# Attention scores of two tiles as 64 queries by 120 key columns in four array quadrants, in place of 32 queries by 88 columns in eight

## The chip, the cores and the metric

The kernel runs on one core of one Trainium2 chip. The metric is device microseconds (us) from one launch, and the median of several runs is compared. A profiled execution gives a trace beside its time; the time of that execution and its span (first to last instruction) are given below.

## The reference

The program is a block of attention with a local window and block summaries, followed by a feed-forward layer. The batch is 4, there are 8 heads of 64 channels and 768 positions.

```
k_sum = k.reshape(B, H, nb, 32, D).max(axis=3)      # 24 summary keys per head
v_sum = v.reshape(B, H, nb, 32, D).mean(axis=3)
scores_l = scale * q @ k^T                          # kept where |i - j| < 16, else -1e9
scores_s = scale * q @ k_sum^T + log(32)
a = softmax(concat([scores_l, scores_s]))
x = a @ concat([v, v_sum])                          # all heads side by side: 3072 x 512
out = max(x @ w_in, 0)**2 @ w_out                   # 512 -> 2048 -> 512
```

A query sees 31 positions around itself and the 24 summaries. So 64 neighbouring queries need 96 local keys and 24 summaries (120 columns), and 32 neighbouring queries need 64 local keys and 24 summaries (88 columns).

## The kernel before, in words

**Tiles.** The 3072 rows are 24 tiles of 128 queries, six to a batch entry. Two tiles make one of 12 chunks of the feed-forward layer. Heads lie in four pairs: of a pair, one head holds partitions 0 to 63 and the other 64 to 127.

**Two stages.** The text START is an order written out by hand: its tokens are loads, attention steps of tiles 0 to 5, the preparation of the weights (32-bit words split into a high and a low part) and the feed-forward of chunks 0 and 1. Behind START a regular loop runs chunks 2 to 11. A chunk is eight slots. In a slot TensorE does the first product for two blocks of the hidden layer (`ffn1`, L392, 24 matmuls of 256 columns) and then the second product of the two blocks of the slot before (`ffn2`, L433, 12 matmuls of 512 columns). Between the two, ScalarE and VectorE make the square of the positive part in a high and a low piece (`squares`, L400 to L414).

**The attention of the next two tiles is spread over the eight slots** by `period`, which appends each step to the lists `before`, `after` and `last` of a slot. For tiles a and a+1: `softmax` (per head, VectorE subtracts the mask and takes the maximum, L307, and ScalarE takes the exponential, L315), `inverse`, `norm` (GpSimd multiplies by the reciprocal sum, four heads in one instruction, L331), `turn` (twelve VectorE transposes of 32-row blocks for each tile, L348). At the end of slot 7 stands what is called a **visit** here: TensorE does `outputs` of both tiles (L362) and the scores of the next two tiles, and `split_x` makes the high and low part of the outputs (ScalarE L376, VectorE L379) for the next chunk's L392.

**Two forms of scores.** Tiles 4 and 5, in START, use `scores` (L254, the matmul's line is 262): for each pair four matmuls, 64 channels by 64 queries by 120 columns, on the four quadrants of the array. Tiles 6 to 23 use `scores_by_group` (L267, the matmul's line is 279): for each pair eight matmuls, 64 channels by 32 queries by 88 columns, on two row halves and four column quarters. Each of these float32 matmuls leaves two records in the trace, each with a weight load of its own. A visit does two tiles, so 64 matmuls, or 128 records. There are nine such visits, the first at the end of START (tiles 6 and 7). The tenth visit has outputs alone.

**Keys.** For tiles from 6 on, a load brings 120 columns per pair and half, of which the middle 24 are room for the maxima; `place_k` writes these from `ksums`. For tiles 4 and 5 the columns lie in five runs of 24, and the maxima are the fifth run. All loads are issued from SyncE in the order of the code.

Of the kernel before, what the change touches and what calls it, by code (L numbers as in the profile page):

```python
# [73 lines left out]
def attn_ffn_kernel(ctx: ExitStack, tc: tile.TileContext, q, k, k0, kt, v, vt, v0, w, masks, gmasks, ident, mean, out):  # L74
# [20 lines left out]
    def by_run(g):
        return k_sb[g % 2].rearrange("a (n s p k) -> a n s p k", n=5, s=2, p=NPAIR)

    def by_pair(g):
        return k_sb[g % 2].rearrange("a (s p k) -> a s p k", s=2, p=NPAIR)
# [154 lines left out]
    def scores(g, p0, p1):  # L254


        if g not in s_ps:
            s_ps[g] = [bank[r].rearrange("a (p k) -> a p k", p=NPAIR) for r in range(2)]
        for p in range(p0, p1):
            for r, s in ((0, 0), (1, 1), (0, 1), (1, 0)):  # L260
                rs, ss = slice(r * 64, r * 64 + 64), slice(s * 64, s * 64 + 64)
                nc.tensor.matmul(  # L262
                    s_ps[g][r][ss, p, 0:NK], lhsT=q_sb[g % 2][rs, s, p, :], rhs=by_run(g)[rs, :, s, p, :],
                    start=True, stop=True,
                )

    def scores_by_group(g):  # L267

        for t in (g, g + 1):
            s_ps[t] = [bank[t % 2 * 2 + r].rearrange("a (p k) -> a p k", p=NPAIR) for r in range(2)]
            for p in range(NPAIR):
                for r, i in ((0, 0), (1, 2), (0, 1), (1, 3), (0, 2), (1, 0), (0, 3), (1, 1)):
                    s, u = divmod(i, 2)
# [1 line left out]
                    nc.tensor.matmul(  # L279
                        s_ps[t][r][i * GQ : i * GQ + GQ, p, 0:GK], lhsT=q_sb[t % 2][rs, s, p, u * GQ : u * GQ + GQ],  # L280
                        rhs=by_pair(t)[rs, s, p, u * GQ : u * GQ + GK], start=True, stop=True,
                    )

    def scores_kt(g, p0, p1):

        if g not in s_ps:
            s_ps[g] = [bank[r].rearrange("a (p k) -> a p k", p=NPAIR) for r in range(2)]
        for p in range(p0, p1):
            for k0, k1 in ((0, 96), (96, NK)):
                for r, s in ((0, 0), (1, 1), (0, 1), (1, 0)):  # L290
# [3 lines left out]
                    nc.tensor.matmul(  # L294
                        s_ps[g][r][ss, p, k0:k1], lhsT=q_sb[g % 2][rs, s, p, :], rhs=keys, start=True, stop=True
                    )

    def mask_max(g, h):

        t = g % NT  # L300
# [6 lines left out]
        nc.vector.tensor_tensor_reduce(  # L307
            out=e_sb[:, h, 0:n], in0=s_ps[g][h % 2][:, h // 2, 0:n], in1=m, scale=-scale, scalar=3.0e38,
            op0=ALU.add, op1=ALU.min, accum_out=nmx[half][:, i : i + 1],
        )  # L310

    def exponentials(g, h):
        half, i = divmod(h, 4)
        e = e_sb[:, h, 0 : NK if g < FROM_GROUPS else GK]
        nc.scalar.activation(e, e, AF.Exp, bias=nmx[half][:, i : i + 1], scale=-1.0, accum_out=sm[half][:, i : i + 1])  # L315
# [12 lines left out]
    def norm(g, half, eng):  # L328
        n = NK if g < FROM_GROUPS else GK
        e = e_sb[:, half * 4 : half * 4 + 4, 0:n]  # L330
        eng.tensor_mul(out=e, in0=e, in1=sm[half].unsqueeze(2).to_broadcast([P, 4, n]))  # L331
# [8 lines left out]
    def turn(g, n0, n1):  # L340

        blocks = [
            (i, c, j) for i in range(4) for c, j in (((0, 0), (32, 1), (64, 3)) if i % 2 == 0 else ((0, 1), (32, 3), (GK - 32, 2)))
        ]
        for i, c, j in blocks[n0:n1]:
            nc.vector.transpose(  # L348
                out=pT[g % 2][j * 32 : j * 32 + 32, :, i * 32 : i * 32 + 32],
                in_=e_sb[i * 32 : i * 32 + 32, :, c : c + 32],  # L350
            )
# [3 lines left out]
    def outputs(g):  # L355
        xp = bank[2 if g < FROM_GROUPS - 1 else free[0] if g < FROM_GROUPS else 5 - g % 2]
        x_ps[g] = xp = xp.rearrange("a (p k) -> a p k", p=NPAIR)

        for s in range(2):
            for h in range(H):  # L360
                o = (h % 2) * 64
                nc.tensor.matmul(  # L362
                    xp[o : o + 64, h // 2, s * 64 : s * 64 + 64],
                    lhsT=v_sb[g % 2][:, s, h * 64 : h * 64 + 64],
                    rhs=pT[g % 2][:, h, s * 64 : s * 64 + 64],
                    start=True, stop=True,
                )
# [168 lines left out]
    def load(what, i):  # L536
# [17 lines left out]
        elif what == "gm":  # L554
            nc.sync.dma_start(out=gmask_sb, in_=gmasks.rearrange("m q c -> q m c"))
        elif what == "id":
            nc.sync.dma_start(out=id_sb, in_=ident)
        else:
            nc.sync.dma_start(out=mean_sb, in_=mean)

    def begin(op, i, j, eng):
# [15 lines left out]
        elif op == "S":  # L577
            if i < FROM_GROUPS:
                (scores_kt if i < FROM_KT else scores)(i, 2 * j, 2 * j + 2)
            else:  # L580
                scores_by_group(i)
# [81 lines left out]
def _group_masks(m):  # L663
    g = np.empty((3, P, GK), np.float32)
    for i in range(P // GQ):
        rows = slice(i * GQ, (i + 1) * GQ)
        runs = [m[:, rows, 0:32], m[:, rows, 32:64], m[:, rows, 64:96]]
        runs = [runs[0], runs[1], m[:, rows, 96:]] if i % 2 == 0 else [runs[1], m[:, rows, 96:], runs[2]]
        g[:, rows] = np.concatenate(runs, axis=2)
    return g  # L670


# [7 lines left out]
def _layouts(q, k, v):  # L680
# [14 lines left out]
    return {
        "q": np.ascontiguousarray(qd).reshape(B, NT, P, 2, NPAIR, 64),
        "k": kg.reshape(B, NT, P, 2 * NPAIR * NK),
        "k0": np.ascontiguousarray(
            kd[0, FROM_KT:].reshape(FROM_GROUPS - FROM_KT, P, 2, NPAIR, 4, NB).transpose(0, 1, 4, 2, 3, 5)
        ),  # L700
# [29 lines left out]
```

## Time and profile before

| what | value |
|---|---|
| median of 3 runs | 624.66 us (624.01 to 625.30) |
| profiled execution | 623.76 us |
| its span | 622.0 us |
| mean granted TensorE clock | 0.992 |
| busy: TensorE matmuls, weight loads | 96%, 86% of the span |
| busy: VectorE, ScalarE, GpSimd | 62%, 43%, 14% |
| bytes moved | 62.33 MB, 100 GB/s |

In the rows below, PE is TensorE's matmul stream and PEld its stream of weight loads, which overlaps the first. DVE is VectorE, ACT ScalarE, POOL GpSimd, SP SyncE. A row of a timeline gives the start, the duration, the engine, the source line, the instruction with its operands, and how many were merged into the row; a bracket at its end is the idle time of the engine just before, and what ended it. "issue" there means that the profile shows nothing for which the engine waited. A row of a group gives the count, then the busy time and the mean of one in ns. A row of windows gives the stretch, its length, and for each engine the busy time with the count of instructions, then the granted clock, the share of the DMA engines and GB/s.

### The profile page before, as it was taken

To read this page: it belongs to the slowest core of one execution; us is meant where nothing else is said; L and a number is where in the kernel's file an instruction comes from. 1 tells how busy PE (TensorE), PEld (TensorE's weight loads), DVE (VectorE), ACT (ScalarE), POOL (GpSimd) and SP (SyncE) were. 2 spreads that over 40 slices of the span, in tenths; PEclk is the share of its full clock that TensorE was granted. 3 is DMA by queue.
4 is the path that set the end of the run, shared out by engine and by line. 5 is a ranking of instruction groups with operands and counts; after the bars stand their busy time and mean duration, and the time that the engine had idled before them with its cause. 6 is when DMAs were issued, how large, how long until landed. Compare 5 with 4: busy or idle time off the path is not lost.

```text
span 622.0 us, 14129 instructions
## 1 busy us (share of the span) xinstructions
PE 595.3 (96%) x5792; PEld 536.8 (86%) x5792; DVE 385.8 (62%) x1073; ACT 266.5 (43%) x706; POOL 89.4 (14%) x83
## 2 busy tenths in 40 slices
PE   2699999999999999999999999999999999999997
PEld 2588888989989999999989988989998998998996
DVE  4889989767645855865653873784763663663221
ACT  2778887333424424425425334334334433332222
POOL 2555762002000000002000000000200000000000
PEclk9979999999999999999999999999999999999999
DMA  8999610545004404203302510600500500200000
GB/s 289 368 355 317 244 70 21 195 161 171 1 2 135 150 3 132 102 2 109 125 2 65 170 52 29 205 1 4 181 2 2 183 0 3 85 2 1 35 1 34
DMA packets 20256, 62.33 MB, mean 100 GB/s; under 512 B 3168, under 2 KB 3296, under 8 KB 18144
## 3 DMA queue, kind: packets, MB, share of 16 engines
q1 hardware_dynamic: 20192, 61.43, 29.8%
q8 instruction: 45, 0.74, 0.5%
q14 instruction: 19, 0.16, 0.1%
HBM read 55.13 MB, written 6.29 MB: 99 GB/s over the span
## 4 chain that ended last, share of the span: by engine, by line
PE 91%; DMA 3%; DVE 2%; ACT 1%; issue 1%; SPq 1%; POOL 0%; DVEq 0%; POOLq 0%
PE o_ps L433 41%; PE ph L392 40%; PE ph L362 3%; PE s_ps L279 2%; PE s_ps L392 2%; DMA w_raw<-in_w 2%; DMA q_sb<-in_q 2%; PE ph L337 1%; PE s_ps L294 1%; PE s_ps L362 1%; DVE w_sb L248 0%; PE o_ps L149 0%; ACT w_sb L123 0%; PE s_ps L262 0%; SPq L172 0%
## 5 line engine op out<-in xcount | busy, mean ns | idle before, releaser
L392 PE MATMUL ph<-xh,w_sb 128*128 128x256 f32 x1448 | 255.8, 279 | 1.5 <-issue 0.9
L433 PE MATMUL o_ps<-w_sb,gh 128*128 128x512 f32 x768 | 238.0, 391 | 0.0
L392 PEld LDWEIGHTS ph<-xh,w_sb 128*128 128x128 f32 x1448 | 225.5, 189 | 9.8 <-issue 1.1
L392 PE MATMUL ph<-xl,w_sb 128*128 128x256 f32 x724 | 201.1, 278 | 0.0
L411 DVE TENSOR_TENSOR ph<-ph,r 128x512 f32<-128x512 f32 (+1 forms) x101 | 64.7, 642 | 152.2 <-ACT r L400 151.6
L433 PEld LDWEIGHTS o_ps<-w_sb,gh 128*128 128x128 f32 x768 | 137.1, 188 | 24.8 <-issue 0.2
L433 PE MATMUL o_ps<-w_sb,gl 128*128 128x512 f32 x384 | 151.4, 394 | 0.8 <-DVE gl L414 0.8
L400 ACT ACTIVATE r<-ph 128x512 f32<-128x512 f32 (+1 forms) x91 | 51.7, 569 | 206.4 <-PE ph L392 206.3
L392 PEld LDWEIGHTS ph<-xl,w_sb 128*128 128x128 f32 x724 | 136.7, 189 | 0.0
L315 ACT ACTIVATE e_sb<-e_sb,nmx 128x88 f32<-128x88 f32 (+1 forms) x192 | 69.8, 365 | 77.3 <-DVE nmx L307 77.3
L348 DVE STREAM_TRANSPOSE pT<-e_sb 32x256 f32<-32x256 f32 x216 | 94.1, 436 | 3.4 <-POOL e_sb L331 0.4
L433 PEld LDWEIGHTS o_ps<-w_sb,gl 128*128 128x128 f32 x384 | 72.3, 188 | 15.6 <-DVE gl L414 1.3
L331 POOL TENSOR_TENSOR e_sb<-e_sb,sm 128x352 f32<-128x352 f32 (+1 forms) x43 | 35.6, 833 | 334.1 <-DVE sm L325 190.3
L414 DVE TENSOR_TENSOR gl<-ph,gh 128x512 fp32r<-128x512 f32 (+1 forms) x101 | 64.2, 636 | 10.5 <-DVE ph L411 0.5
L406 ACT ACTIVATE gh<-r 128x512 fp32r<-128x512 f32 (+1 forms) x112 | 63.9, 571 | 8.7 <-DVE r L402 5.2
L241 POOL TENSOR_TENSOR w_raw<-w_raw 128x1024 int32<-128x1024 int32 x16 | 35.3, 2215 | 24.4 <-ACT w_raw L233 7.5
L315 ACT ACTIVATION_READ_ACCUMULATOR e_sb<-e_sb,nmx 128x1 f32 x192 | 36.0, 188 | 0.0
L307 DVE CUSTOM_DVE_ANT_0 e_sb<-s_ps,gmask_sb 128x88 f32<-128x88 f32 x144 | 27.4, 244 | 0.4
L379 DVE TENSOR_TENSOR xl<-ph,xh 128x512 fp32r<-128x512 f32 x19 | 13.1, 691 | 22.7 <-ACT xh L376 22.7
L324 DVE TENSOR_SCALAR sm<-sm 128x4 f32<-128x4 f32 x48 | 14.9, 311 | 14.7 <-ACT e_sb L315 14.6
L376 ACT CAST xh<-ph 128x512 fp32r<-128x512 f32 x19 | 11.1, 585 | 26.9 <-PE ph L362 26.9
L362 PEld LDWEIGHTS ph<-pT,v_sb 128*64 128x64 f32 x608 | 18.6, 138 | 3.9 <-issue 3.3
(67 smaller groups left out, 394.5 us busy)
## 6 DMA issues: line engine op xcount, KB each, us to landing
w_raw<-in_w SPq DMA_DIRECT2D x16, 1024.0 KB, 13.9
v_sb<-in_v SPq DMA_DIRECT2D x24, 384.0 KB, 5.1
k_sb<-in_k SPq DMA_DIRECT2D x18, 480.0 KB, 6.1
kv<-in_kt SPq DMA_DIRECT2D x16, 384.0 KB, 3.3
q_sb<-in_q SPq DMA_DIRECT2D x24, 256.0 KB, 5.4
out<-ob SPq DMA_DIRECT2D x24, 256.0 KB, 2.1
kv<-in_vt SPq DMA_DIRECT2D x12, 384.0 KB, 4.1
vn<-in_v SPq DMA_DIRECT2D x2, 768.0 KB, 11.0
```

What stands on the lines that cost most here:

```text
L241: nc.gpsimd.tensor_tensor(out=hi, in0=hi, in1=lo, op=ALU.add)
L307: nc.vector.tensor_tensor_reduce(out=e_sb[:, h, 0:n], in0=s_ps[g][h % 2][:, h // 2, 0:n], in1=m, scale=-scale, scalar=3.0e38, op0=ALU.add, ...
L315: nc.scalar.activation(e, e, AF.Exp, bias=nmx[half][:, i : i + 1], scale=-1.0, accum_out=sm[half][:, i : i + 1])
L331: eng.tensor_mul(out=e, in0=e, in1=sm[half].unsqueeze(2).to_broadcast([P, 4, n]))
L348: nc.vector.transpose(out=pT[g % 2][j * 32 : j * 32 + 32, :, i * 32 : i * 32 + 32], in_=e_sb[i * 32 : i * 32 + 32, :, c : c + 32],)
L362: nc.tensor.matmul(xp[o : o + 64, h // 2, s * 64 : s * 64 + 64], lhsT=v_sb[g % 2][:, s, h * 64 : h * 64 + 64], rhs=pT[g % 2][:, h, s * 64 ...
L392: nc.tensor.matmul(ph, lhsT=w_sb[f][:, w, cc * P : (cc + 1) * P], rhs=x[c][:, cc, :], start=(n == 0), stop=(n == 3 * NC4 - 1))
L400: nc.scalar.activation(r, ph, AF.Relu)
L406: nc.scalar.activation(gh, r, AF.Square)
L411: nc.vector.tensor_mul(out=ph, in0=ph, in1=r)
L414: nc.vector.tensor_sub(out=gl, in0=ph, in1=gh.bitcast(F32))
L433: nc.tensor.matmul(o_ps[c][tt], lhsT=g_[:, ts_], rhs=w_sb[f][:, w, DM:], start=(first and n == 0), stop=(last and n == 2),)
```

## The change

`scores_by_group` is gone, and tiles 6 to 23 use `scores`, so that a visit has 32 matmuls of 64 queries by 120 columns (64 records) where it had 64 of 32 by 88 (128 records). The keys of all tiles are loaded in four runs of 24 columns, with the maxima as a fifth run behind them, so a load of keys brings 768 columns where it brought 960. The mask of 88 columns and its load are gone. The maximum, the exponential and the product with the reciprocal work on 120 columns where they worked on 88, and the blocks that `turn` transposes lie at other columns, as many as before. Which banks of PSUM the scores use stays as it was, as does the order of the steps.

```diff
-GQ = 32
-GK = 64 + NB
-FROM_GROUPS = 6
+FROM_PAIRS = 6
...
-KT0 O5 PK6 VT0 PK7 XH5a S6.0 XL5v
+KT0 O5 PK6 VT0 PK7 XH5a S6.0 S6.1 XL5v S7.0 S7.1
...
-    k_sb = [const.tile([P, 2 * NPAIR * NK], F32, name=f"k_sb{i}") for i in range(2)]
+    k_sb = [const.tile([P, 5, 2, NPAIR, NB], F32, name=f"k_sb{i}") for i in range(2)]
...
-        if g < FROM_GROUPS:
-            nc.sync.dma_start(out=by_run(g)[:, 0:4], in_=k0[g - FROM_KT])
-        else:
-            nc.sync.dma_start(out=k_sb[g % 2], in_=k[g // NT, g % NT])
+        nc.sync.dma_start(out=k_sb[g % 2][:, 0:4], in_=k[g // NT, g % NT])
...
-        dst = by_run(g)[:, 4] if g < FROM_GROUPS else by_pair(g)[:, :, :, 64:GK]
-        copy(eng, dst, ksums[g // NT % 2].unsqueeze(1).to_broadcast([P, 2, NPAIR, NB]))
+        copy(eng, k_sb[g % 2][:, 4], ksums[g // NT % 2].unsqueeze(1).to_broadcast([P, 2, NPAIR, NB]))
...
         if g not in s_ps:
-            s_ps[g] = [bank[r].rearrange("a (p k) -> a p k", p=NPAIR) for r in range(2)]
+            n = g % 2 * 2 if g >= FROM_PAIRS else 0
+            s_ps[g] = [bank[n + r].rearrange("a (p k) -> a p k", p=NPAIR) for r in range(2)]
         for p in range(p0, p1):
             for r, s in ((0, 0), (1, 1), (0, 1), (1, 0)):
                 rs, ss = slice(r * 64, r * 64 + 64), slice(s * 64, s * 64 + 64)
                 nc.tensor.matmul(
-                    s_ps[g][r][ss, p, 0:NK], lhsT=q_sb[g % 2][rs, s, p, :], rhs=by_run(g)[rs, :, s, p, :],
+                    s_ps[g][r][ss, p, 0:NK], lhsT=q_sb[g % 2][rs, s, p, :], rhs=k_sb[g % 2][rs, :, s, p, :],
                     start=True, stop=True,
                 )
-    def scores_by_group(g):
-        for t in (g, g + 1):
-            s_ps[t] = [bank[t % 2 * 2 + r].rearrange("a (p k) -> a p k", p=NPAIR) for r in range(2)]
-            for p in range(NPAIR):
-                for r, i in ((0, 0), (1, 2), (0, 1), (1, 3), (0, 2), (1, 0), (0, 3), (1, 1)):
-                    s, u = divmod(i, 2)
-                    rs = slice(r * 64, r * 64 + 64)
-                    nc.tensor.matmul(
-                        s_ps[t][r][i * GQ : i * GQ + GQ, p, 0:GK], lhsT=q_sb[t % 2][rs, s, p, u * GQ : u * GQ + GQ],
-                        rhs=by_pair(t)[rs, s, p, u * GQ : u * GQ + GK], start=True, stop=True,
-                    )
...
         nc.vector.tensor_tensor_reduce(
-            out=e_sb[:, h, 0:n], in0=s_ps[g][h % 2][:, h // 2, 0:n], in1=m, scale=-scale, scalar=3.0e38,
+            out=e_sb[:, h, 0:NK], in0=s_ps[g][h % 2][:, h // 2, 0:NK], in1=m, scale=-scale, scalar=3.0e38,
...
-        e = e_sb[:, h, 0 : NK if g < FROM_GROUPS else GK]
+        e = e_sb[:, h, 0:NK]
...
-        n = NK if g < FROM_GROUPS else GK
-        e = e_sb[:, half * 4 : half * 4 + 4, 0:n]
-        eng.tensor_mul(out=e, in0=e, in1=sm[half].unsqueeze(2).to_broadcast([P, 4, n]))
+        e = e_sb[:, half * 4 : half * 4 + 4, 0:NK]
+        eng.tensor_mul(out=e, in0=e, in1=sm[half].unsqueeze(2).to_broadcast([P, 4, NK]))
...
-            (i, c, j) for i in range(4) for c, j in (((0, 0), (32, 1), (64, 3)) if i % 2 == 0 else ((0, 1), (32, 3), (GK - 32, 2)))
+        blocks = [(i, j) for i in range(4) for j in ((0, 1, 3) if i % 2 == 0 else (1, 2, 3))]
...
-            last[7].append(lambda: scores_by_group(a + 2))
+            last[7] += [lambda g=g: scores(g, 0, NPAIR) for g in (a + 2, a + 3)]
```

How the instructions stand on TensorE at the second visit, before (the end of the last `ffn2`, the outputs of two tiles, the scores of two tiles, the first `ffn1`; the count at a row's end is of matmuls, each of which the trace shows as two records where operands are float32 and not rounded):

```order
L433 MATMUL o_ps<-w_sb,gl 128x512
L362 MATMUL ph<-pT_81,v_sb_76 64x64 x16
L362 MATMUL ph<-pT_82,v_sb_77 64x64 x16
L279 MATMUL s_ps<-k_sb_74,q_sb_78 32x88 x32
L279 MATMUL s_ps<-k_sb_75,q_sb_79 32x88 x32
L392 MATMUL ph<-xh,w_sb 128x256 x2
L392 MATMUL ph<-xl,w_sb 128x256
```

The same place of the changed kernel, where line 398 is `ffn2`, 327 `outputs`, 249 `scores` and 357 `ffn1`:

```order
L398 MATMUL o_ps<-w_sb,gl 128x512
L327 MATMUL ph<-pT_80,v_sb_75 64x64 x16
L327 MATMUL ph<-pT_81,v_sb_76 64x64 x16
L249 MATMUL s_ps<-k_sb_73,q_sb_77 64x120 x16
L249 MATMUL s_ps<-k_sb_74,q_sb_78 64x120 x16
L357 MATMUL ph<-xh,w_sb 128x256 x2
L357 MATMUL ph<-xl,w_sb 128x256
```

The place in the stream is the same; a row of scores holds half as many matmuls, each twice as tall and 120 columns wide. On VectorE at the first visit, the end of START, before (k_sb is written by `place_k`, then come the low part of the outputs and the first maxima of tile 6):

```order
L180 TENSOR_REDUCE ksum_84<-kv 128x24
L123 COPY k_sb_74<-ksum_84 128x8x24
L185 TENSOR_REDUCE vsum<-kv 128x24
L188 TENSOR_SCALAR vsum<-vsum 128x24
L123 COPY k_sb_75<-ksum_84 128x8x24
L379 TENSOR_TENSOR xl<-ph,xh 128x4x128
L307 ISA e_sb,nmx<-s_ps,gmask_sb 128x88
```

And in the changed kernel:

```order
L167 TENSOR_REDUCE ksum_83<-kv 128x24
L113 COPY k_sb_73<-ksum_83 128x192
L172 TENSOR_REDUCE vsum<-kv 128x24
L175 TENSOR_SCALAR vsum<-vsum 128x24
L113 COPY k_sb_74<-ksum_83 128x192
L344 TENSOR_TENSOR xl<-ph,xh 128x4x128
L277 ISA e_sb,nmx<-s_ps,mask_sb 128x120
```

Here too the places are the same; the copies write one run where they wrote eight pieces, and the maxima read 120 columns.

More of the change, by code (lines that the diff above doesn't have):

```diff
@@ L63 @@
 F1.19 CA14a GL17v MU18 LO15a GL18v F1.20 SU14v RE19a F2.17 SQ19 AD15 MU19 CA13a GL19v RE20v F2.18 E5.7 MU20 SQ20
-SU13v E5.6 F2.19 E5.1 GL20v E5.2 CA15v F2.20 E5.0 SU15v E5.3 F1.21 E5.4 NR5.0 L:gm L:kw2 E5.5 N5.0v F1.22 RE21a NR5.1
+SU13v E5.6 F2.19 E5.1 GL20v E5.2 CA15v F2.20 E5.0 SU15v E5.3 F1.21 E5.4 NR5.0 L:kw2 E5.5 N5.0v F1.22 RE21a NR5.1
 N5.1v SQ21 MU21 F1.23 RE22a GL21v SQ22 MU22 GL22v F2.21 RE23a SQ23 MU23 GL23v F1.24 KT2 F2.22 VT2 RE24a SQ24
@@ L68, with attn_ffn_kernel @@
 MU29 F1.31 RE30a GL29v VT3 F2.27 RE31a MU30 L:kw0 MU31 F2.28 SQ30 GL30v F2.29 SQ31 GL31v T5.0 T5.1 TC5.0v TC5.1a
-KT0 O5 PK6 VT0 PK7 XH5a S6.0 XL5v
+KT0 O5 PK6 VT0 PK7 XH5a S6.0 S6.1 XL5v S7.0 S7.1
 """
 @with_exitstack
-def attn_ffn_kernel(ctx: ExitStack, tc: tile.TileContext, q, k, k0, kt, v, vt, v0, w, masks, gmasks, ident, mean, out):
+def attn_ffn_kernel(ctx: ExitStack, tc: tile.TileContext, q, k, kt, v, vt, v0, w, masks, ident, mean, out):
     nc = tc.nc
@@ L87, in attn_ffn_kernel @@
     mask_sb = const.tile([P, 3, NK], F32, name="mask_sb")
-    gmask_sb = const.tile([P, 3, GK], F32, name="gmask_sb")
     id_sb = const.tile([P, P], F32, name="id_sb")
     mean_sb = const.tile([P, 52], F32, name="mean_sb")
-    k_sb = [const.tile([P, 2 * NPAIR * NK], F32, name=f"k_sb{i}") for i in range(2)]
[L95 to L99, printed above, removed]
+    k_sb = [const.tile([P, 5, 2, NPAIR, NB], F32, name=f"k_sb{i}") for i in range(2)]
     v_sb = [const.tile([P, 2, DM], F32, name=f"v_sb{i}") for i in range(2)]
@@ L262, in scores @@
                 nc.tensor.matmul(
-                    s_ps[g][r][ss, p, 0:NK], lhsT=q_sb[g % 2][rs, s, p, :], rhs=by_run(g)[rs, :, s, p, :],
+                    s_ps[g][r][ss, p, 0:NK], lhsT=q_sb[g % 2][rs, s, p, :], rhs=k_sb[g % 2][rs, :, s, p, :],
                     start=True, stop=True,
                 )
-    def scores_by_group(g):
-        for t in (g, g + 1):
-            s_ps[t] = [bank[t % 2 * 2 + r].rearrange("a (p k) -> a p k", p=NPAIR) for r in range(2)]
-            for p in range(NPAIR):
-                for r, i in ((0, 0), (1, 2), (0, 1), (1, 3), (0, 2), (1, 0), (0, 3), (1, 1)):
-                    s, u = divmod(i, 2)
-                    rs = slice(r * 64, r * 64 + 64)
-                    nc.tensor.matmul(
-                        s_ps[t][r][i * GQ : i * GQ + GQ, p, 0:GK], lhsT=q_sb[t % 2][rs, s, p, u * GQ : u * GQ + GQ],
-                        rhs=by_pair(t)[rs, s, p, u * GQ : u * GQ + GK], start=True, stop=True,
-                    )
     def scores_kt(g, p0, p1):
         if g not in s_ps:
-            s_ps[g] = [bank[r].rearrange("a (p k) -> a p k", p=NPAIR) for r in range(2)]
+            n = g % 2 * 2 if g >= FROM_PAIRS else 0
+            s_ps[g] = [bank[n + r].rearrange("a (p k) -> a p k", p=NPAIR) for r in range(2)]
         for p in range(p0, p1):
@@ L300, in mask_max @@
         t = g % NT
-        n = NK if g < FROM_GROUPS else GK
-        m = (mask_sb if g < FROM_GROUPS else gmask_sb)[:, 0 if t == 0 else 2 if t == NT - 1 else 1, :]
+        m = mask_sb[:, 0 if t == 0 else 2 if t == NT - 1 else 1, :]
         half, i = divmod(h, 4)
@@ L320, in softmax @@
             mask_max(g, h)
-            exponentials(g, h)
+            exponentials(h)
     def inverse(half):
@@ L326, in inverse, with norm @@
         del nmx[half]
-    def norm(g, half, eng):
-        n = NK if g < FROM_GROUPS else GK
-        e = e_sb[:, half * 4 : half * 4 + 4, 0:n]
-        eng.tensor_mul(out=e, in0=e, in1=sm[half].unsqueeze(2).to_broadcast([P, 4, n]))
+    def norm(half, eng):
+        e = e_sb[:, half * 4 : half * 4 + 4, 0:NK]
+        eng.tensor_mul(out=e, in0=e, in1=sm[half].unsqueeze(2).to_broadcast([P, 4, NK]))
     def turn_pe(g, half, tp):
@@ L340, in turn @@
     def turn(g, n0, n1):
-        blocks = [
-            (i, c, j) for i in range(4) for c, j in (((0, 0), (32, 1), (64, 3)) if i % 2 == 0 else ((0, 1), (32, 3), (GK - 32, 2)))
-        ]
-        for i, c, j in blocks[n0:n1]:
+        blocks = [(i, j) for i in range(4) for j in ((0, 1, 3) if i % 2 == 0 else (1, 2, 3))]
+        for i, j in blocks[n0:n1]:
             nc.vector.transpose(
                 out=pT[g % 2][j * 32 : j * 32 + 32, :, i * 32 : i * 32 + 32],
-                in_=e_sb[i * 32 : i * 32 + 32, :, c : c + 32],
+                in_=e_sb[i * 32 : i * 32 + 32, :, j * 32 : j * 32 + 32],
             )
@@ L355, in outputs @@
     def outputs(g):
-        xp = bank[2 if g < FROM_GROUPS - 1 else free[0] if g < FROM_GROUPS else 5 - g % 2]
+        xp = bank[2 if g < FROM_PAIRS - 1 else free[0] if g < FROM_PAIRS else 5 - g % 2]
         x_ps[g] = xp = xp.rearrange("a (p k) -> a p k", p=NPAIR)
@@ L492, in period @@
             return before, after, last
-        if a > FROM_GROUPS:
+        if a > FROM_PAIRS:
             last[1] += [lambda: load_v(a), lambda: load_v(a + 1)]
@@ L499, in period @@
         before[1].append(lambda: softmax(a, 3, 6))
-        after[1] += [lambda: softmax(a, 6, 8), lambda: inverse(0), lambda: norm(a, 0, nc.gpsimd)]
-        before[2] += [lambda: inverse(1), lambda: norm(a, 1, nc.gpsimd)]
+        after[1] += [lambda: softmax(a, 6, 8), lambda: inverse(0), lambda: norm(0, nc.gpsimd)]
+        before[2] += [lambda: inverse(1), lambda: norm(1, nc.gpsimd)]
         after[2].append(lambda: turn(a, 0, 3))
@@ L506, in period @@
         after[4].append(lambda: softmax(a + 1, 4, 6))
-        before[5] += [lambda: softmax(a + 1, 6, 8), lambda: inverse(0), lambda: norm(a + 1, 0, nc.gpsimd)]
-        before[5] += [lambda: inverse(1), lambda: norm(a + 1, 1, nc.gpsimd)]
+        before[5] += [lambda: softmax(a + 1, 6, 8), lambda: inverse(0), lambda: norm(0, nc.gpsimd)]
+        before[5] += [lambda: inverse(1), lambda: norm(1, nc.gpsimd)]
         before[6].append(lambda: turn(a + 1, 0, 5))
@@ L553, in load @@
             nc.sync.dma_start(out=mask_sb, in_=masks.rearrange("m q c -> q m c"))
-        elif what == "gm":
-            nc.sync.dma_start(out=gmask_sb, in_=gmasks.rearrange("m q c -> q m c"))
         elif what == "id":
@@ L577, in begin @@
         elif op == "S":
[L578 to L581, printed above, removed]
+            (scores_kt if i < FROM_KT else scores)(i, 2 * j, 2 * j + 2)
         elif op == "TT":
@@ L584, in begin @@
         elif op == "E":
-            exponentials(i, j)
+            exponentials(j)
         elif op == "NR":
@@ L588, in begin @@
         elif op == "N":
-            norm(i, j, eng)
+            norm(j, eng)
         elif op == "T":
@@ L660, in _masks @@
     return m
[L663 to L670, printed above, removed]
 def _mean():
@@ L685, in _layouts @@
     vp[:, :, WINDOW : WINDOW + S] = v
-    kd = np.zeros((B, NT, 2, D, 2, NPAIR, 96), k.dtype)
-    kg = np.zeros((B, NT, 2, D, 2, NPAIR, NK), k.dtype)
+    kd = np.zeros((B, NT, 2, D, 4, 2, NPAIR, NB), k.dtype)
     vd = np.zeros((B, NT, 96, 2, H, D), v.dtype)
@@ L691, in _layouts @@
             o = t * P + s * 64
-            kd[:, t, :, :, s] = kp[:, :, o : o + 96].reshape(B, NPAIR, 2, 96, D).transpose(0, 2, 4, 1, 3)
+            kd[:, t, :, :, :, s] = kp[:, :, o : o + 96].reshape(B, NPAIR, 2, 4, NB, D).transpose(0, 2, 5, 3, 1, 4)
             vd[:, t, :, s] = vp[:, :, o : o + 96].transpose(0, 2, 1, 3)
-    kg[..., 0:64], kg[..., GK:] = kd[..., 0:64], kd[..., 64:]
     return {
         "q": np.ascontiguousarray(qd).reshape(B, NT, P, 2, NPAIR, 64),
[L697 to L700, printed above, removed]
+        "k": kd.reshape(B, NT, P, 4, 2, NPAIR, NB),
         "kt": np.ascontiguousarray(k.transpose(0, 1, 3, 2)).reshape(B, NPAIR, P, S),
@@ L716 @@
     arrays["masks"] = _masks()
-    arrays["gmasks"] = _group_masks(arrays["masks"])
     arrays["ident"] = np.eye(P, dtype=np.float32)
```

2 lines of the change are left out of this document (1 added, 1 removed).

## The prediction

> **What bounds the kernel now.** I read the page first: the share of TensorE and the chain that ended last.
>
> ```profile
> span 622.0 us, 14129 instructions
> PE 595.3 (96%) x5792; PEld 536.8 (86%) x5792; DVE 385.8 (62%) x1073; ACT 266.5 (43%) x706; POOL 89.4 (14%) x83
> PE 91%; DMA 3%; DVE 2%; ACT 1%; issue 1%; SPq 1%; POOL 0%; DVEq 0%; POOLq 0%
> ```
>
> TensorE is busy for 96% of the span and carries 91% of the chain. Time is won or lost where TensorE's stream gets shorter or longer, or where it stops. So I next cut the regular loop by windows, each from the start of one visit's outputs to the next one's. First two windows without a stop, then the four that are longer, then the sum over all eight.
>
> ```profile
> 273.99:321.74 47.75, 47.75 (x481) 43.35 (x481) 28.40 (x86) 18.62 (x54) 4.78 (x7) 1.00 0.23 77
> 467.39:515.13 47.74, 47.74 (x482) 43.34 (x481) 26.81 (x82) 18.53 (x54) 3.10 (x4) 1.00 0.18 60
> 177.30:226.23 48.93, 48.05 (x481) 43.52 (x480) 30.96 (x88) 18.50 (x54) 3.10 (x4) 1.00 0.29 91
> 321.74:370.35 48.61, 47.94 (x481) 43.34 (x480) 30.95 (x88) 18.51 (x54) 3.10 (x4) 1.00 0.29 92
> 370.35:419.64 49.29, 48.05 (x481) 43.47 (x481) 30.97 (x88) 18.50 (x54) 3.10 (x4) 1.00 0.23 75
> 515.13:563.36 48.23, 48.05 (x481) 43.45 (x481) 26.81 (x82) 18.03 (x52) 3.10 (x4) 1.00 0.10 29
> sum 386.06, PE 383.09 PEld 347.18 DVE 234.24 ACT 147.82 POOL 28.13; mean PE 47.89 PEld 43.40 DVE 29.28 ACT 18.48 POOL 3.52
> ```
>
> The granted clock is 1.00 in all. A period without a stop is 47.75 us, eight of them would be 382.0, and they take 386.06: **4.06 us are lost**, in four of the eight (1.18, 0.86, 1.54 and 0.48). The timeline of TensorE shows where. First an undisturbed visit: outputs, scores, first matmul of the next chunk. Then the broken ones: the rows at which the scores, or in the first of them the matmuls just behind, go on after a gap.
>
> ```profile
> 419.64 2.08 PE L362 MATMUL ph<-pT,v_sb 128*64 128x64 f32 x64
> 421.65 1.67 PE L279 MATMUL s_ps<-k_sb,q_sb 64*32 64x88 f32 x128
> 423.25 0.50 PE L392 MATMUL ph<-xh,w_sb 128*128 128x256 f32 x2
> ...
> 182.41 0.40 PE L392 MATMUL ph<-xh,w_sb 128*128 128x256 f32 x2 [0.88 <-issue]
> ...
> 323.75 1.29 PE L279 MATMUL s_ps<-k_sb,q_sb 64*32 64x88 f32 x95
> 325.72 0.56 PE L279 MATMUL s_ps<-k_sb,q_sb 64*32 64x88 f32 x33 [0.67 <-issue]
> ...
> 372.37 1.63 PE L279 MATMUL s_ps<-k_sb,q_sb 64*32 64x88 f32 x125
> 375.24 0.34 PE L279 MATMUL s_ps<-k_sb,q_sb 64*32 64x88 f32 x3 [1.24 <-issue]
> ...
> 517.14 1.24 PE L279 MATMUL s_ps<-k_sb,q_sb 64*32 64x88 f32 x89
> 518.57 0.73 PE L279 MATMUL s_ps<-k_sb,q_sb 64*32 64x88 f32 x39 [0.18 <-issue]
> ```
>
> The gaps end on "issue": no semaphore, no data. They break the row of scores at another matmul each time (after 95, 125, 89). What they have in common is a count. Matmuls from the end of one gap to the end of the next, and the queue that brings instructions:
>
> ```profile
> 182.41:325.71 143.30, 142.63 (x1404) 1.00 0.26 83
> 325.71:375.24 49.53, 48.29 (x512) 1.00 0.29 90
> 375.24:518.57 143.33, 143.15 (x1405) 1.00 0.20 66
> q8 instruction: 45, 0.74, 0.5%
> ```
>
> Each matmul has one weight load (5792 of both), so the stretches are 2808, 1024 and 2810 instructions, which is 11, 4 and 11 times 256 but for a handful (2816, 1024, 2816; I take the rest to be waits, which these counts leave out). The queue moved 0.74 MB in 45 packets, 16.4 KB each, and the 11584 instructions are 45 times 257. So TensorE's program comes in blocks of 256 instructions, that is 128 matmuls with their loads, and the gaps lie on borders of blocks. The border before the gap at 325.72 lies 128 matmuls back, at the 31st of the 64 of outputs, which ran at 321.74 + 31 x 2.02/64 = 322.72. From there to the restart are 3.0 us. The same working gives 372.28 to 375.24, again 3.0, and 515.92 to 518.57, 2.65. A block that runs through in less than about 3 us has to wait for the next one. Outputs and scores together are 192 matmuls in 3.6 us, so a block that lies well inside them runs through faster than that. In the rest of the loop 128 matmuls take over 14 us.
>
> [...] If the gaps were something else, they would stay; that is the second rival.
>
> **The change part by part.**
>
> *Scores on TensorE.* Both forms are in the trace, as are their followers: the new form ran for tiles 4 and 5 in START.
>
> ```profile
> L279 PE MATMUL s_ps<-k_sb,q_sb 64*32 64x88 f32 x1152 | 16.0, 242 | 2.3 <-issue 2.1 <-DVE k_sb L123 0.3
> L262 PE MATMUL s_ps<-k_sb,q_sb 64*64 64x120 f32 x64 | 2.3, 272 | 0.0
> 54.82 1.05 PE L262 MATMUL s_ps<-k_sb,q_sb 64*64 64x120 f32 x32
> 55.80 1.15 PE L362 MATMUL s_ps<-pT,v_sb 128*64 128x64 f32 x32
> ...
> 80.75 0.64 PE L262 MATMUL s_ps<-k_sb,q_sb 64*64 64x120 f32 x16
> 81.33 0.50 PE L392 MATMUL ph<-xh,w_sb 128*128 128x256 f32 x2
> ```
>
> The means of one are no price, since four or eight run at once. By starts, the old form takes 423.25 - 421.65 = 1.60 us for 128 records, 12.5 ns each. The new one takes 0.98 us for 32 and 0.58 for 16, so 25 ns for each further record: 64 of them take 0.98 + 32 x 0.025 = 1.78. Half the count at twice the price: the array has four pieces at work where it had eight. I take **+0.2 us a visit**. From below, 64 x 25 = 1.60 with no cost at the start would be +0.0. From above, two runs of 32 that share nothing are 1.96, +0.36. At the first visit the tiles run apart, because the second waits for its keys:
>
> ```profile
> 137.77 0.96 PE L279 MATMUL s_ps<-k_sb,q_sb 64*32 64x88 f32 x64 [0.26 <-DVE k_sb L123]
> ```
>
> There the first tile's 0.1 goes into the wait of 0.26, and the second tile's 0.1 counts. In all 8 x 0.2 + 0.1 = **+1.7 us** (0 to 3.0).
>
> If the old form kept all eight pieces streaming, cost would go by columns per piece, 120 x 64 / 4 against 88 x 128 / 8, and the new form would take 1.36 times 1.60, or +0.58 a visit instead of +0.2. The starts of L262 say that it does not; it is the third rival.
>
> [...]
>
> *The gaps.* A visit of the loop now holds 64 matmuls of outputs in 2.02 us and 64 of scores in 1.78: exactly one block's worth, in 3.8 us. Any block that is not wholly in these two holds matmuls of L392 or L433, which are slower. So no block runs through in under 3.8 us, against the 3.0 that a refill needs: **-4.06 us**. The slack is 0.8 us. If it is not enough for one block, a gap like the smallest, 0.48, stays (-3.6). The borders also fall elsewhere, since a period is 128 instructions shorter, but that matters only if a refill needs over 3.8.
>
> *Softmax.* The steps over 120 columns are in the trace as well.
>
> ```profile
> L307 DVE CUSTOM_DVE_ANT_0 e_sb<-s_ps,gmask_sb 128x88 f32<-128x88 f32 x144 | 27.4, 244 | 0.4
> L307 DVE CUSTOM_DVE_ANT_0 e_sb<-s_ps,mask_sb 128x120 f32<-128x120 f32 x48 | 11.3, 276 | 5.1 <-PE s_ps L262 1.6 <-PE s_ps L294 1.4 <-PE ph L337 0.8
> L315 ACT ACTIVATE e_sb<-e_sb,nmx 128x88 f32<-128x88 f32 x144 | 51.4, 358 | 65.5 <-DVE nmx L307 65.5
> L315 ACT ACTIVATE e_sb<-e_sb,nmx 128x120 f32<-128x120 f32 x48 | 18.5, 387 | 11.9 <-DVE nmx L307 11.9
> L331 POOL TENSOR_TENSOR e_sb<-e_sb,sm 128x352 f32<-128x352 f32 x36 | 27.7, 773 | 319.2 <-DVE sm L325 178.5 <-ACT e_sb L315 140.5
> L331 POOL TENSOR_TENSOR e_sb<-e_sb,sm 128x480 f32<-128x480 f32 x7 | 7.9, 1137 | 14.9 <-DVE sm L325 11.8 <-ACT w_raw L226 1.4 <-ACT gh L406 1.0
> 413.71 3.14 DVE L348 STREAM_TRANSPOSE pT<-e_sb 32x256 f32<-32x256 f32 x7
> 417.68 0.70 DVE L411 TENSOR_TENSOR ph<-ph,r 128x512 f32<-128x512 f32 x1 [0.83 <-ACT r L400]
> ```
>
> Per period and 16 heads VectorE gets 16 x 32 ns = 0.5 us more, ScalarE 16 x 29 = 0.5, GpSimd 4 x 0.364 = 1.5, where they are busy for 31, 18.6 and 4.8 of 47.75 at most. The one link that is tight in order is `norm` to `turn`: VectorE stands in line at the transposes until GpSimd is through, 0.36 us later than now, and behind them wait the squares. The last transposes end at 416.85, 0.83 us before VectorE's next work and 2.8 us before the outputs at 419.64 read them. I price it at nothing; without that cover it would be 18 tiles x 0.36 = 6.5 us.
>
> *Loads and copies.* Keys of 384 KB instead of 480 and no mask load: TensorE has no wait for keys' transfers in the loop. The copies of maxima move the same 192 elements. Nothing.
>
> **The sum.** 622.0 - 4.06 + 1.7 = 619.6 us of span. The profiled time of 623.76 is 1.8 above its span, so 621.4 there. The median of the runs is 0.9 higher, 624.66, and the same difference of 2.36 gives **622.3 us**, 0.38% less.
>
> **The rivals.**
>
> 1. *Refills need more than 3.8 us when other transfers run beside them*, so about half the gaps stay. For: the slack is 0.8 us. Against: the three borders that can be timed give 2.65 to 3.0, at DMA shares from 0.10 to 0.29. 624.66 - 2.03 + 1.7 = 624.3.
> 2. *The gaps belong to the visit and not to the count*, so they stay and only the dearer matmuls are felt: 624.66 + 1.7 = 626.4, slower. It decides if over 85% of the 4.06 stay. Against it stand the multiples of 256 and the visits without any gap.
> 3. *Eight pieces are worth their number*, +0.58 a visit: 624.66 - 4.06 + 8.5 x 0.58 = 625.5, no change. Against it stand the starts of L262.
> 4. *A record costs the same in both forms*, because issue is the limit: 0.80 us a visit, 624.66 - 4.06 - 8.5 x 0.8 = 613.8. Against it again L262, 25 ns and not 12.5.
> 5. *The longer norm makes the transposes late*: 622.3 + 6.5 = 628.8. Against it stand the 0.83 and 2.8 us.
>
> **How the numbers follow.** Forecast 0.78, rivals in order 0.07, 0.05, 0.04, 0.03, 0.03. I count 0.2%, 1.25 us, as about what a measurement of this kernel can tell from no change. Faster: nearly all of the forecast and rival 4, 0.79. The same: rivals 1 and 3 and the forecast's upper edge, 0.13. Slower: rivals 2 and 5, 0.08. The forecast's own bounds are 624.66 - 4.06 + 0 = 620.6 and 624.66 - 3.6 + 3.0 = 624.1, and the three runs lie 0.6 to each side of their median; not all of it adds up, so 620.9 to 624.5, which takes in rival 1 and leaves out less than 2 in 10.
>
> **What would show each step.** Right: windows from visit to visit of 47.95 us, all alike within 0.1; no gap on "issue" inside or just behind a visit; 1.8 us from the first score to the next chunk's first matmul; 576 records of 64x120 in the loop; some 41 packets on the instruction queue. Wrong: gaps at the visits in a period of 256 instructions (rival 1) or at the old places (2); 2.2 or 0.8 us for the scores (3, 4); outputs that wait for VectorE (5).

## The result, and the profile after

The changed kernel takes 621.03 us (median of 6 runs, 620.03 to 621.48) and the kernel before, in the same comparison, 624.67 (624.01 to 627.41). The ratio of the runs is 0.9933, with a 95% interval of 0.9913 to 0.9953, so the gain is 0.5% to 0.9%, 2.9 to 5.4 us. The forecast was a gain of 2.36 us (0.38%) and a time of 622.3; the direction is right, the gain larger. In the traces the span fell from 622.0 to 619.3 us, by 2.7.

Three executions, the traced one of *before_again* and one each of two variants, took 1588 to 3453 us, the traced one with slow matmuls from end to end (672 ns in the mean at L392, where the first trace has 279), and all comparisons below leave them out.

The head of the page of the changed kernel, with its chain and its instruction queue:

```profile
span 619.3 us, 12979 instructions
PE 596.7 (96%) x5216; PEld 538.7 (87%) x5216; DVE 391.9 (63%) x1073; ACT 270.3 (44%) x706; POOL 97.2 (16%) x83
...
q8 instruction: 41, 0.67, 0.5%
...
PE 92%; DMA 3%; DVE 2%; ACT 1%; SPq 1%; issue 0%; POOL 0%; DVEq 0%; POOLq 0%
```

TensorE is as busy as before, its records fell by 576, the packets of instructions from 45 to 41, and the 1% of "issue" has left the chain. The loop by windows from visit to visit: the longest, one of the others, and the sum of all eight.

```profile
225.03:272.98 47.95, 47.95 (x418) 43.51 (x417) 31.68 (x88) 18.93 (x54) 3.95 (x4) 1.00 0.22 72
...
368.86:416.80 47.94, 47.94 (x418) 43.50 (x417) 31.68 (x88) 18.94 (x54) 3.95 (x4) 1.00 0.21 72
...
sum 383.52, PE 383.52 PEld 348.03 DVE 239.76 ACT 151.26 POOL 34.99; mean PE 47.94 PEld 43.50 DVE 29.97 ACT 18.91 POOL 4.37
```

All eight are 47.93 to 47.95 us, and TensorE is busy for the whole 383.52. Where the traces differ by 2.7 us: the first visit starts 0.31 earlier (135.38 to 135.07), the stretch from it to the second is 0.10 longer, the eight periods are 2.54 shorter, and what follows is 0.06 longer. The timeline of one visit (outputs, scores, what follows):

```profile
416.80 2.09 PE L327 MATMUL ph<-pT,v_sb 128*64 128x64 f32 x64
418.81 1.87 PE L249 MATMUL s_ps<-k_sb,q_sb 64*64 64x120 f32 x64
420.61 0.50 PE L357 MATMUL ph<-xh,w_sb 128*128 128x256 f32 x2
```

The scores take 420.61 - 418.81 = 1.80 us, where the old form takes 1.60.

### The profile page after: what moved, and what is told of

The parts are those of the page before. It is cut to its first block, busy times and chain, and to the rows that moved or that the text cites. A ratio compares the mean times of both kernels' runs of the same rounds, so it can differ in the third digit from the quotient of the medians.

```text
span 619.3 us, 12979 instructions
## 1 busy us (share of the span) xinstructions
PE 596.7 (96%) x5216; PEld 538.7 (87%) x5216; DVE 391.9 (63%) x1073; ACT 270.3 (44%) x706; POOL 97.2 (16%) x83
## 4 chain that ended last, share of the span: by engine, by line
PE 92%; DMA 3%; DVE 2%; ACT 1%; SPq 1%; issue 0%; POOL 0%; DVEq 0%; POOLq 0%
PE o_ps L398 42%; PE ph L357 40%; PE s_ps L249 3%; PE ph L327 3%; PE s_ps L357 2%; DMA w_raw<-in_w 2%; DMA q_sb<-in_q 1%; PE ph L306 1%; PE s_ps L265 1%; PE s_ps L327 1%; DVE w_sb L234 0%; PE o_ps L136 0%; ACT w_sb L113 0%; SPq L159 0%; SPq L117 0%
## 5 line engine op out<-in xcount | busy, mean ns | idle before, releaser
L285 ACT ACTIVATE e_sb<-e_sb,nmx 128x120 f32<-128x120 f32 x192 | 73.7, 385 | 78.2 <-DVE nmx L277 78.2
L300 POOL TENSOR_TENSOR e_sb<-e_sb,sm 128x480 f32<-128x480 f32 x43 | 43.3, 1011 | 324.8 <-DVE sm L295 179.4
L277 DVE CUSTOM_DVE_ANT_0 e_sb<-s_ps,mask_sb 128x120 f32<-128x120 f32 x192 | 43.4, 277 | 5.2 <-PE s_ps L249 1.6
L344 DVE TENSOR_TENSOR xl<-ph,xh 128x512 fp32r<-128x512 f32 x19 | 13.1, 691 | 22.7 <-ACT xh L341 22.7
L294 DVE TENSOR_SCALAR sm<-sm 128x4 f32<-128x4 f32 x48 | 16.3, 339 | 14.8 <-ACT e_sb L285 14.8
```

The source lines that it names most:

```text
L277: nc.vector.tensor_tensor_reduce(out=e_sb[:, h, 0:NK], in0=s_ps[g][h % 2][:, h // 2, 0:NK], in1=m, scale=-scale, scalar=3.0e38, op0=ALU.ad ...
```

## The experiments

**Does the gap follow the border of a block?** The kernel *shift* puts 128 instructions more into START, so that all later borders lie half a block away from where they were.

```diff
+        for n in range(32):
+            nc.tensor.matmul(
+                ps[0:32, 256:272], lhsT=mean_sb[:, 0:32], rhs=vn[0][:, 0, 0:16], start=True, stop=True
+            )
```

> The kernel before with 32 short matmuls more (64 records and their loads, 128 instructions) at the end of the means of the values in START; nothing else is changed, and their result is not read. All later borders of 256 instructions move by 128 against the work. Theory (the gaps lie on borders of blocks of 256 instructions, and a block that runs through in under 3 to 4 us waits): the gaps leave the visits 2, 5, 6 and 9 and come up at 3, 4 and 8, and just behind visit 1, 3 to 5 us in all. Rival (the gaps belong to a visit, by its data or its transfers): they stay at visits 2, 5, 6 and 9. The span tells nothing apart: 622 to 625 us by both.

It took 622.81 us in one run (span 621.0). Its eight periods, of visits 2 to 9 in order:

```profile
177.18:224.91 47.73, 47.73 (x481) 1.00 0.28 93
224.91:273.41 48.50, 47.97 (x482) 1.00 0.23 76
273.41:322.10 48.69, 47.70 (x481) 1.00 0.22 76
322.10:369.83 47.73, 47.73 (x481) 1.00 0.29 94
369.83:417.59 47.76, 47.76 (x482) 1.00 0.23 77
417.59:465.80 48.21, 48.06 (x481) 1.00 0.18 60
465.80:514.60 48.80, 48.05 (x481) 1.00 0.18 59
514.60:562.35 47.75, 47.75 (x481) 1.00 0.10 29
sum 385.17, PE 382.76; mean PE 47.84
```

And the rows of TensorE's timeline that follow a gap:

```profile
138.62 0.28 PE L396 MATMUL ph<-xh,w_sb 128*128 128x256 f32 x1 [0.32 <-issue]
...
228.81 0.42 PE L283 MATMUL s_ps<-k_sb,q_sb 64*32 64x88 f32 x19 [0.53 <-issue]
...
278.07 0.40 PE L396 MATMUL ph<-xh,w_sb 128*128 128x256 f32 x2 [0.99 <-issue]
...
421.03 0.39 PE L283 MATMUL s_ps<-k_sb,q_sb 64*32 64x88 f32 x16 [0.15 <-issue]
...
470.18 0.35 PE L283 MATMUL s_ps<-k_sb,q_sb 64*32 64x88 f32 x6 [0.75 <-issue]
```

Visits 2, 5, 6 and 9, which had the gaps, are clean; the gaps stand at visits 3, 4 and 8, just behind visit 1, and a small one at visit 7 that was not foreseen. In all the gaps cost 3.2 us in the eight periods (385.17 against 382.0) and 0.6 behind visit 1 (42.54 us from visit 1 to visit 2, where it was 41.92). One more, of 0.8 us, came up in START. The visits' work, data and transfers are the same as before, so the gaps belong to the borders. The queue of instructions agrees: in both traces a packet of 16.4 KB lands on it 1.2 to 1.5 us ahead of every one of these restarts.

**Is it the count of instructions, or how fast they run?** Two kernels do every score of the loop twice. In the old form (*double_old*, of the kernel before):

```diff
-            for p in range(NPAIR):
+            for p in (*range(NPAIR), *range(NPAIR)):
```

> The kernel before with every matmul of the 32 by 88 scores done twice over (256 records a visit in place of 128, the same results written again). Theory: the scores alone now hold two blocks that run through in 1.6 us each, so nearly every visit has a gap of 1.5 to 2.5 us or two smaller ones, 17 to 19 us in all nine; with 9 x 1.44 us for the matmuls the span is 622 + 13 + 14 = 649 us. Rival (gaps belong to a visit): the gaps stay at 4 us, span 635 us.

In the new form (*double_new*, of the changed kernel):

```diff
-        for p in range(p0, p1):
+        for p in (*range(p0, p1), *(range(p0, p1) if g >= FROM_PAIRS else ())):
```

> The changed kernel with every matmul of the 64 by 120 scores of tiles 6 to 23 done twice over (128 records a visit, as many as the kernel before has, the same results written again). Theory: 256 instructions of this form take over 3.2 us, and a block with any other work takes longer, so there is no gap: 619.3 + 9 x 1.64 = 634 us, periods alike within 0.1 us. Rival (what counts is how many instructions a visit has, not how fast they run): the gaps of the kernel before come back, at the same four visits, 4 us: 638 us.

*double_old* took 670.41 us (span 668.6), 20 more than the theory's 649. What TensorE waited for, and a visit with two gaps:

```profile
PE s_ps L279 <- issue: 20.9, 12, 2.7
...
PE ph L392 <- issue: 1.8, 1, 1.8
```

```profile
185.38 1.73 PE L279 MATMUL s_ps<-k_sb,q_sb 64*32 64x88 f32 x131
188.96 1.63 PE L279 MATMUL s_ps<-k_sb,q_sb 64*32 64x88 f32 x125 [1.84 <-issue]
190.52 0.51 PE L392 MATMUL ph<-xh,w_sb 128*128 128x256 f32 x2
...
192.96 0.40 PE L392 MATMUL ph<-xh,w_sb 128*128 128x256 f32 x2 [1.82 <-issue]
```

There are 13 gaps, every visit has one or two, and they come to 22.7 us of idle time. From one restart to the next, 188.96 to 192.96, lie 4.0 us (3.8 to 4.1 in the four visits with two gaps). I read this as the time of a refill when the next one is asked for at once. The rest of the excess is the clock, of which more below. The rival's 635 us is out.

*double_new* took 637.33 us (span 635.6; 634 was expected, 1.0 of the difference lies ahead of the first visit). Two of its periods and the sum:

```profile
180.06:229.66 49.60, 49.60 (x481) 1.00 0.26 86
229.66:279.24 49.58, 49.58 (x481) 1.00 0.21 70
...
sum 396.66, PE 396.66; mean PE 49.58
```

It has as many matmuls in a visit and in a period as the kernel before, so a border comes as often, and there is not one gap: 47.94 + 1.64 = 49.58. So it is not the count, but 256 instructions that run through faster than the next 256 arrive (those of the scores in 1.6 us in *double_old*, in 3.4 us here).

**Would the old form do without the gaps, if its instructions were spread?** *split* keeps the old form and moves half of the scores ahead of the second product of slot 7.

```diff
+        for do in middle:
+            do()
         done = finish()
...
-            last[7].append(lambda: scores_by_group(a + 2))
+            middle[7].append(lambda: scores_by_group(a + 2, 1))
+            last[7].append(lambda: scores_by_group(a + 3, 1))
```

> The kernel before with the scores of the first tile of a visit moved ahead of the second product of slot 7 (between its 24 and its 12 matmuls), in the old form; the scores of the second tile stay behind the outputs. As many instructions as before, in the same blocks. Theory: between the two halves lie 12 slow matmuls, no block runs through in under 4 us, and the gaps are gone; two more changes of the array's division cost 0.15 to 0.2 us each, so a period is 48.1 us and the span 622.0 - 4.06 + 2.8 = 620.7 us. Rival (the gaps go with the count of instructions or with the visit): 4 us of gaps stay, span 624.8 us.

It took 624.05 us (median of 12 runs, 622.98 to 626.09), 0.999 of the kernel before (0.997 to 1.001); its span was 621.7, 1.0 over the forecast. Two periods, and the timeline around a visit:

```profile
179.11:227.24 48.13, 48.13 (x481) 1.00 0.29 93
227.24:275.37 48.13, 48.13 (x482) 1.00 0.23 76
```

```profile
223.40 0.96 PE L279 MATMUL s_ps<-k_sb,q_sb 64*32 64x88 f32 x64
224.29 0.72 PE L433 MATMUL o_ps<-w_sb,gh 128*128 128x512 f32 x2
...
227.24 2.08 PE L362 MATMUL ph<-pT,v_sb 128*64 128x64 f32 x64
229.26 0.96 PE L279 MATMUL s_ps<-k_sb,q_sb 64*32 64x88 f32 x64
```

The gaps are gone, and the period is 48.13 as forecast. But parting the scores costs 0.38 a period (48.13 against 47.75), more than the 0.2 of the new form (47.94). Some 0.7 us more were lost between visit 1 and visit 2, where there is no gap; that kind of loss comes up again below. The changed kernel stays the fastest.

**Why the timed gain is larger than the traced one.** The kernels as they are, run again:

> The kernel before, unchanged, for a second trace and more times. The traces gave a difference of 2.7 us between the two kernels, the medians of six runs 3.6. Theory A (START differs from run to run with its first transfers, and the first trace of before was a short one there): the first visit lies between 134.6 and 136.2 us in any trace of either kernel, the gaps again cost 4.0 us within 0.5, and over many runs the kernels differ by 2.5 to 3 us. Rival B (the gaps vary from run to run and mostly cost more than in the first trace): the eight periods sum to 387 us or more in place of 386.06.

> The changed kernel, unchanged, beside the kernel before on the same chip. Both theories: periods of 47.94 us, no gap. Theory A: times 2.5 to 3 us under those of the kernel before, and as widely spread as those. Rival B: 3.5 us or more under them, and closer together.

> The kernel before, a third trace. Theory A: sum of the eight periods 386.1 us within 0.5. Rival B: 387 us or more in this trace or in the second.

> The changed kernel, a second trace beside the one of after_again. Both theories: eight periods of 47.94 us. Theory A: where its span differs from 619.3 us, the difference lies before the first visit.

*after_again* took 621.58 us (median of 6, 620.95 to 622.16) beside 625.43 for the kernel before (17 runs, 622.92 to 627.76): ratio 0.9933 again (0.9917 to 0.9949). The difference of 3.9 us and the narrower spread of the changed kernel (1.2 us against 4.8) are the signs of rival B. The eleven compared runs of *before_again* have a ratio of 0.9996 to the kernel before (0.9978 to 1.0013), as they must. *before_again2* took 627.64 us (span 625.9), *after_again2* 621.72 (619.9). The loop of the changed kernel in the two new traces, from the second visit to the last:

```profile
176.98:560.50 383.52, 383.52 (x3329) 1.00 0.20 67
```

```profile
177.74:561.26 383.52, 383.52 (x3329) 1.00 0.21 67
```

It repeats to a hundredth. The one of the kernel before does not. The periods of visits 6 and 7 and the sum in *before_again2*, then a stretch behind the gap of visit 6, and the rows from the end of that gap on:

```profile
370.07:422.26 52.19, 50.39 (x481) 45.62 (x480) 30.95 (x88) 18.52 (x54) 3.10 (x4) 0.97 0.22 71
422.26:470.82 48.56, 48.56 (x481) 43.98 (x480) 28.39 (x86) 18.64 (x54) 4.79 (x7) 1.00 0.19 60
...
sum 389.92, PE 386.27 PEld 349.94 DVE 234.24 ACT 147.89 POOL 28.19; mean PE 48.28 PEld 43.74 DVE 29.28 ACT 18.49 POOL 3.52
```

```profile
376.25:379.66 3.41, 3.41 (x19) 0.50 0.03 5
```

```profile
375.52 0.34 PE L279 MATMUL s_ps<-k_sb,q_sb 64*32 64x88 f32 x3 [1.80 <-issue]
...
376.25 0.62 PE L392 MATMUL ph<-xh,w_sb 128*128 128x256 f32 x2
376.66 0.41 PE L392 MATMUL ph<-xl,w_sb 128*128 128x256 f32 x1
376.88 0.63 PE L392 MATMUL ph<-xh,w_sb 128*128 128x256 f32 x2
```

The gap at visit 6 was longer than in the first trace (1.80 us of idle time against 1.24), and behind it TensorE ran for 3.41 us at half its clock, which costs another 1.7. The period lost 4.44 us where it had lost 1.54, and the loop 7.92 against 4.06.

Not all of that is gaps and half clock. The period of visit 7 has no gap, TensorE is busy for all of it at a granted clock of 1.00, and yet it is 0.81 us longer than 47.75. In windows of L392 alone its 192 matmuls take 24.03 us, where in the first trace the same 192 take 23.38. These slower matmuls last from the gap of visit 6 to visit 8. They also run from visit 1 to visit 2 of this trace (0.7 us) and behind the last visit of *before_3* (0.9 us), and in *split* and *double_new*, which have no gap, from visit 1 to visit 2 (0.7 us each). The three traces of the changed kernel have none. What sets them off is not shown.

Three more traces:

> The kernel before, one more trace, to see how much its gaps vary. So far the eight periods summed to 386.06 and 389.92 us, where 382.0 would be without gaps. Theory (gaps vary, typically more than in the first trace; a gap of 2 us or more is followed by a stretch at half the clock): the sum lies between 386 and 390, the long periods are those after visits 2, 5, 6 and 9, and where a gap passes 2 us the granted clock is 0.5 for about 3.4 us. Rival (389.92 was the exception, and the rest of the difference lies in START): 386.1 within 0.5, no half clock.

> As for the trace before it: theory, a sum of the eight periods between 386 and 390 with a mean over all traces near 387.5; rival, 386.1 within 0.5.

> As for the two traces before it: theory, a sum of the eight periods between 386 and 390; rival, 386.1 within 0.5.

They took 623.44, 622.30 and 623.42 us. The sums of their eight periods:

```profile
sum 385.94, PE 382.96; mean PE 47.87
```

```profile
sum 386.13, PE 383.13; mean PE 47.89
```

```profile
sum 386.65, PE 382.97; mean PE 47.87
```

The long periods are at the same four visits, and no half clock came up. So the theory of generally longer gaps holds for one trace in five. The five lose 4.06, 7.92, 3.94, 4.13 and 4.65 us, 4.94 on average; against 383.52 the mean difference of the loops is 3.4 us, the middle one 2.6. The eight periods are not all, since a loss can fall ahead of them or behind. From the first visit to the end the five take 486.6, 491.3, 487.4, 486.7 and 487.3 us, and the changed kernel takes 484.2 in each of its three traces: 3.7 us less on average, 3.1 in the middle. The first of the five, on which the prediction stood, is the shortest.

The last pair asks whether the gaps are longer in runs that leave no trace:

> The kernel with the doubled old scores (13 gaps, 28.6 us in its trace, and five stretches at half the clock), now in many runs. In kernels without a gap the timed runs are 0 to 0.8 us over the traced one; in the kernel before they are 1.2 to 1.8 over most of its traces. Theory (gaps are longer in the timed runs, about 0.3 us each): the median of the runs is 3 us or more over 670.4 us, at like clocks. Rival (what the kernel before has more in its timed runs is no gap): within 1 us of the traced run, but for half-clock stretches, each of which shows as 0.0025 of mean clock and 1.7 us.

> The kernel with the doubled new scores, which has no gap, in many runs beside the other. Both: the median within 1 us of 637.3 us, and spread by 1 to 2 us like the changed kernel.

*double_old_timed* took 663.18 us (median of five, 662.43 to 663.93), 7 us less than the first trace of that kernel and not 3 us more. Its own trace again has 13 gaps, with 21.0 us of idle time, and three stretches at half the clock where there were five. *double_new_timed* took 636.1 us (four runs, 634.45 to 636.48), 1.2 less than its first trace. The theory that untraced gaps are longer falls for this kernel; the rival's limit of 1 us is missed too, since the two stretches that are gone explain only 3.4 of the 7 us.

## Why the prediction was right, and where it failed

**The gaps** were read rightly, and all of them went. That they are refills of the instruction stream, in blocks of 256, was argued from a count in the prediction and is now shown: shifting the stream moved them, doubling a fast form multiplied them, doubling a slow one made none, spreading the instructions took them away. Rival 2 falls with the changed kernel's equal periods. Rival 1 is half right: a refill did take some 3.8 us (3.5 to 4.1, by the pairs below), but the gaps that it derived from this did not come.

**The time of a refill was put too low**, at about 3 us; from restart to restart it is 3.5 to 4.1 in the eight pairs of *double_old* and *double_old_timed*. With a block of outputs and scores in 3.8 us the slack of 0.8 that the prediction named would have been about nothing. That no gap came is then not explained by the prediction's own working, which counted from when the border's instruction ran. The packets suggest that the next block is asked for earlier: the one before the gap at 375.24 starts 0.5 us behind the border's instruction, and behind a restart a packet starts some 1.1 us later, so the request lies some 0.6 us ahead (an estimate). By that lead the block of 3.8 us leaves some 4.4 us for a refill, more than the 3.5 to 4.1 measured (an estimate from these packets). No run here shows the lead itself.

**The price of the new form** was +0.2 us a visit from the rows of START; it is 1.80 - 1.60, and a period is 47.94 where 47.95 was forecast. By the columns per piece, rival 3, it would have been 2.18. Rivals 3 and 4 are out.

**Softmax over 120 columns** costs nothing, as forecast, but the cover is thinner than the prediction thought. VectorE's last transposes and the squares behind them in the changed kernel:

```profile
411.68 3.14 DVE L313 STREAM_TRANSPOSE pT<-e_sb 32x256 f32<-32x256 f32 x7
414.85 0.70 DVE L376 TENSOR_TENSOR ph<-ph,r 128x512 f32<-128x512 f32 x1
```

The transposes end 416.80 - 414.82 = 1.98 us ahead of the outputs, where it was 2.8, and the idle 0.83 us before the squares are gone. The squares themselves start 1.95 us ahead of the outputs, as before (1.96). The delay is 0.8 us and not the 0.36 of the prediction, and the product on GpSimd grew only from 0.78 to 0.99 us in the loop: the reciprocal ahead of it already stands 0.84 us later (10.38 us ahead of the outputs, where it was 11.22). So of the cover of 0.83 us at this place all is used; a further 0.1 us would move the squares, which TensorE reads only in the next slot. Rival 5 did not come.

**The step that failed is the gap term of the sum**, -4.06 us, and with it the last line: "the same difference of 2.36 gives 622.3". It took what the gaps cost in one trace as what they cost in every run. For that pair of traces it was good (2.7 of span, 2.54 of it in the loop where 2.46 was forecast: -4.06 + 8 x 0.2). But the kernel before loses another amount in each execution, 3.9 to 7.9 us in the loop in five traces, since gaps vary, the half clock followed a longer one (1.80 us of idle time in *before_again2*), and stretches of slower matmuls come up, while the three traces of the changed kernel agree to a hundredth there. The trace at hand was the shortest of the five from the first visit on: the gain is 2.4 us against it and 3.7 on average. The range had the same fault, for its lower end let no gaps cost more than 4.06. The median of 621.03 lies just inside it; the time by the ratio, 0.9933 x 624.67 = 620.5, is 0.4 us below.

That much is shown. By the ratios the timed runs differ by 4.2 us, by the medians by 3.6 to 3.9, and the intervals are 2.9 to 5.4 and 3.2 to 5.2, so the 3.7 of the traces lies inside both. How much of it in the timed runs is gaps, half clock or slower matmuls stays open. START shows no difference: the first visit starts at 133.8 to 137.2 us in eight traces with the START of before (the variants counted), 135.1 on average, and at 134.1 to 136.1 in five with the changed one, 135.2 on average. Theory A allowed 134.6 to 136.2, so it missed the spread of START too.

One slip changes no number: the matmuls behind a visit (L392) are not those of the next chunk. The loop counts its periods one slot apart from its chunks, so they are the last slot of the same chunk.

## What to carry to other kernels

In this kernel a gap on "issue" that came at a multiple of 256 instructions was a refill of the engine's program. Where TensorE does many very short instructions in a row, ask how long 256 of them take: here 256 that ran through in 1.6 us stalled (*double_old*), 256 in 3.4 us did not (*double_new*), though a refill took 3.5 to 4.1 us. A form that is 12% slower by itself (1.80 against 1.60 us) and has half the instructions won. Before a forecast of a fraction of a percent, see in more than one trace whether the term that goes away is the same each time.

## What the runs showed of the hardware

**Behind gaps of some 2 us TensorE's granted clock was 0.50 for 3.41 us.** In *before_again2* this followed a gap with 1.80 us of idle time; the rows at 376.25 and 376.88 show three matmuls in 0.63 us, where they take 0.34 elsewhere in the loop. In *double_old* there are five such stretches, each 3.41 us long:

```profile
193.95:197.36 3.41, 3.41 (x16) 0.50 0.03 5
142.75:146.16 3.41, 3.41 (x50) 0.50 0.44 120
296.35:299.76 3.41, 3.41 (x74) 0.50 0.02 5
350.96:354.37 3.41, 3.02 (x43) 0.50 0.03 5
562.59:566.00 3.41, 3.41 (x21) 0.50 0.02 5
sum 17.05, PE 16.66; mean PE 3.33
```

That is 17.05 / 2 = 8.5 us, which with the gaps makes up what the expectation missed. The length of the idle time does not tell the cases apart: the idle 1.84 us that end at 188.96 were not followed by half clock, the 1.82 that end at 192.96 were. In order of time the five begin 51.20, 102.40, 54.61 and 211.63 us apart, within 0.1 of 15, 30, 16 and 62 times their own length of 3.41. What sets them off is not shown.

**Eight small pieces of the array were not twice as fast as four.** Eight records of 88 columns take 8 x 12.5 = 100 ns (1.60 us for 128 in the first trace), four of 120 columns 4 x 25 = 100 (by the rows of START there): the eight pieces pass 704 / 480 = 1.47 times the columns, not 2 times. Each further change between small pieces and the whole array cost about 0.2 us (0.38 a period for two, in *split*).
